# Cosine attention into a leaky-ReLU feed-forward on one core: norms of the second batch moved behind the first batch, two feed-forward groups begun in parts, weights and loads reordered, epsilon added by VectorE

## The chip, the cores and the metric

The kernel runs on one core of a Trainium2 chip. The time is that of one execution on the device, in microseconds (us). The core has five engines with queues of their own: TensorE (PE in the profile), VectorE (DVE), ScalarE (ACT), GpSimd (POOL) and SyncE (SP). Each works through its queue in order; between engines they wait on semaphores.

## The reference

Eight batches of attention with 12 heads, 448 tokens and head dimension 64, with normalised queries and keys, and behind it a feed-forward layer on the 3584 resulting tokens:

```python
q_n = q / (norm(q, axis=-1) + 1e-06)
k_n = k / (norm(k, axis=-1) + 1e-06)
scores = q_n @ k_n.T / tau                     # tau = 0.1
attn = softmax(scores, axis=-1)                # denominator + 1e-09
x = (attn @ v).transpose(0, 2, 1, 3).reshape(8 * 448, 768)
h = x @ w_in                                   # 768 x 2048
out = maximum(0.01 * h, h) @ w_out             # 2048 x 768, float32
```

## The kernel before

**Units of work.** A *slot* is a pair of heads of one batch: six slots to a batch, slots 0 to 11 for the first two batches in one layout ("old"), and from slot 12 (`OLD`) on another layout, in which slots carry queries and keys of two pairs by turns. Two slots of an old batch make one *group* j of four heads, three groups to a batch.

**A slot's path.** `load_qk(s)` issues its DMAs on the SP queue into one of four buffers (`ldp`, `bufs=4`), so slot s+4 can only be loaded once slot s is normalised. `squares(s)` (GpSimd, L208, L201) squares the float32 data; `sums(s)` (VectorE, L222, L216) adds over the head dimension into `ss`; `roots(s)` (ScalarE, L229 to L231) takes the root as Ln and Exp with scale 0.5 and then adds epsilon by an Identity activation; `normalise(s)` (VectorE, L239 and L245 or L255) takes the reciprocal and multiplies into the bf16 tile `qn`; `transposes(s)` turns it (L269 on TensorE and the copy L310 on VectorE for old slots, L291 on VectorE and six stores on SP, L300, for new ones) into `qkT`. `hold(x)` is a GpSimd copy of one column that waits for the norm (L580), so that what follows it on GpSimd does not start earlier.

**Attention.** `scores(s, kis)` multiplies key tiles against all queries (L331) into two PSUM banks, and ScalarE takes the exponential with scale 1/tau (L340); tile 3 of a pair of slots holds the last 64 keys of both. `totals(j)` multiplies the exponentials with ones (L351) and takes Ln and Exp with scale -1 on ScalarE (L362, L363); `products(j, e)` multiplies with the values (L351); `scale(j, e)` (VectorE, L382) writes their product into block 2j+e of six of `xT`. New slots use `quad_tiles` (L402, L408), `group_products` (L427) and `group_scale` (L452).

**Feed-forward.** Chunk c of tokens is 384 columns for an even c and 512 for an odd one. `first(c, m)` multiplies six blocks of `w_in` with `xT` (L474) and puts the leaky ReLU (ScalarE, L480) into `hT`; 16 groups m per chunk. `second(c, ts, half)` multiplies 16 blocks of `hT` with one half of `w_out` (L502), copies the result (VectorE, L513) and stores it. Weights and values come by GpSimd's DMA queue (`load_w_in`, `load_w_out`, `load_v`, `load_v_rem`, `load_vq`).

**Order.** It is written out by hand; the program keeps it engine by engine. `fill(n)` issues n matmuls whose results are not used. The first batch is the loop `for s in range(NPAIR)` (six steps): each step issues the scores of slot s, normalises and transposes slot s+1, loads slot s+5, squares slot s+3, and sums and takes the root for slot s+2; in odd steps the remaining value product and the scaling of an earlier group stand between, in even steps that group's totals and first value product stand behind the transposes. Then `attend(j)` does the last group, and a hand-written prelude (L674 to L712) prepares slots 7 to 10 of the second batch between 13 of the 16 first groups of chunk 0 (`feed_groups`). The table `opened` (L718) orders the rest of the second batch and the rest of chunk 0: its row i names tiles of scores and the slot that is prepared ahead. From L764 on, visits of three tiles each are filled with feed-forward work by cost.

PSUM has eight banks; `banks` deals the oldest, in the first batch score tiles from banks 0 to 3 and everything else from 4 to 7 (`deals["apart"]`).

Of the kernel before, what the change touches and what calls it, by code (L numbers as in the profile page):

```python
# [8 lines left out]
F32 = mybir.dt.float32  # L9
# [7 lines left out]
def kernel(  # L17
# [146 lines left out]
    def load_v_rem(b, heads=range(4)):  # L164
        if b >= B:
            return
        r = v[b, :, MAIN:S].rearrange("(j g) p d -> g p j d", g=4)
        for g in heads:
            lo = 64 * (g // 2)
            gp.dma_start(out=vrb[b % 2][lo : lo + 64, :, g], in_=r[g])  # L170
# [55 lines left out]
    def roots(s):  # L226
        if s >= NSLOT:
            return
        nc.scalar.activation(ss[s], ss[s], func=AF.Ln, bias=tiny)  # L229
        nc.scalar.activation(ss[s], ss[s], func=AF.Exp, scale=0.5)  # L230
        nc.scalar.activation(ss[s], ss[s], func=AF.Identity, bias=eps)  # L231

    qn = {}

    def normalise(s):
        if s >= NSLOT:
            return
        r = smp.tile([128, 14], F32, name="r")
        nc.vector.reciprocal(r, ss[s])  # L239
        if s >= OLD:  # L240


            qn[s] = qnp.tile([128, 7, D, 2], BF16, name="qn")
            t, n = ("(m e)", "(e m)")[s % 2], 2
            nc.vector.tensor_tensor(  # L245
                qn[s].rearrange("p m d e -> p m e d"),
                raw[s].rearrange(f"p ({t[1:-1]} d) -> p m e d", e=n, d=D),
                r.rearrange(f"p {t} -> p m e", e=n).unsqueeze(3).to_broadcast([128, 7, 2, D]),
                op=ALU.mult,
            )  # L250
            return
        qn[s] = qnp.tile([128, 7, 2, D], BF16, name="qn")
        for x, lo, hi, r0 in ((raw[s][0], 0, 4, 0), (raw[s][1], 4, 7, 8)):
            nt = hi - lo
            nc.vector.tensor_tensor(  # L255
                qn[s][:, lo:hi],
                x.rearrange("p h t d -> p t h d"),
                r[:, r0 : r0 + 2 * nt].rearrange("p (h t) -> p t h", h=2)
                .unsqueeze(3).to_broadcast([128, nt, 2, D]),
                op=ALU.mult,  # L260
            )
# [203 lines left out]
    def chunk_cols(c):  # L465
        return (0, MAIN) if c % 2 == 0 else (MAIN, 512)

    def first(c, m):
        c0, n = chunk_cols(c)
        if m == 0:  # L470
            hT[c] = htp.tile([128, MT, 512], BF16, name="hT")
        pm = banks(1)
        for kt in range(KT):
            nc.tensor.matmul(  # L474
                out=pm[:, :n],
                lhsT=w_in_sb[:, kt, m * 128 : (m + 1) * 128],
                rhs=xT[c // 2][:, kt, c0 : c0 + n],
                start=(kt == 0), stop=(kt == KT - 1),
            )
        nc.scalar.activation(out=hT[c][:, m, :n], in_=pm[:, :n], func=AF.Prelu, alpha=0.01)  # L480

    osb = {}
# [65 lines left out]
    load_qk(3)  # L548
    tiny = cpool.tile([128, 1], F32, name="tiny")
    nc.vector.memset(tiny, 1e-18)  # L550
    eps = cpool.tile([128, 1], F32, name="eps")
    nc.vector.memset(eps, 1e-6)
    warm = pep.tile([128, 2 * S], BF16, name="pe")[:, 0:512]
    nc.vector.memset(warm, 1.0)  # L554
    ones = cpool.tile([128, 32], BF16, name="ones")
# [22 lines left out]
    def hold(x):  # L578
        seen = smp.tile([128, 1], F32, name="seen")
        gp.tensor_copy(out=seen, in_=x)  # L580
# [34 lines left out]
    for s in range(NPAIR):  # L615
        j = s // 2 - 1 if s >= 2 else None
        even = s % 2 == 0
        n = s + 2 if s and s + 2 <= NPAIR + 1 else None
        if s == 1:
            roots(2)  # L620
        scores(s, (0,))
        if j is not None and not even:
            products(j, 1)
        scores(s, (1,))
        fill(2)
        if n and n <= NPAIR:
            sums(n, (0,))
        normalise(s + 1)
        load_qk(s + 5)
        if j is not None and not even:  # L630
            scale(j, 0)
        hold(qn[s + 1][:, 6, 0, 0:1])
        squares(s + 3)
        if s == 0:
            sums(2)
            load_v_rem(0, range(2, 4))
        if not even:
            load_v(s // 2 + 1)
        if s != 1 and s < 5:
            load_w_in(max(s - 1, 0))  # L640
        if s == 5:
            load_v_rem(1)
        if n:
            sums(n, (1,) if n <= NPAIR else (0, 1))
        scores(s, (2,))
        if not even or s == 0:
            fill(2)
        if not even:
            scores(s, (3,))
        transposes(s + 1)  # L650
        if not even or s == 0:
            fill(2)
        if n:
            roots(n)
        if j is not None and not even:
            scale(j, 1)
        if j is not None and even:
            totals(j)
            products(j, 0)

    def attend(j):
        totals(j)
# [7 lines left out]
    deals["apart"] = False  # L670
    deals["width"] = 64
    s, j = NPAIR, NQ - 1
    attend(j)
    scores(s, (0, 1))  # L674
    feed_groups(0, 1)
    normalise(s + 1)
    load_qk(s + 5)
    load_w_out(0)
    hold(qn[s + 1][:, 6, 0, 0:1])
    squares(s + 3)  # L680
    sums(s + 2)
    feed_groups(0, 3)
    transposes(s + 1)
    roots(s + 2)
    feed_groups(0, 2)
    scores(s, (2,))
    scores(s + 1, (0,))
    normalise(s + 2)
    load_qk(s + 6)
    hold(qn[s + 2][:, 6, 0, 0:1])  # L690
    squares(s + 4)
    load_v(s // 2 + 1)
    load_w_out(1)
    sums(s + 3)
    roots(s + 3)
    feed_groups(0, 2)
    scores(s + 1, (1, 2))
    normalise(s + 3)
    load_qk(s + 7)
    feed_groups(0, 1)  # L700
    transposes(s + 2)
    sums(s + 4)
    feed_groups(0, 2)
    roots(s + 4)
    scores(s + 1, (3,))
    normalise(s + 4)
    load_qk(s + 8)
    hold(qn[s + 4][:, 6, 0, 0:1])
    squares(s + 5)
    feed_groups(0, 1)  # L710
    transposes(s + 3)
    feed_groups(0, 1)  # L712

# [13 lines left out]
    for i, (at, tiles, ahead) in enumerate(opened):  # L729
        share = (sum(g[0] for g in queue[:-1]) + sum(costs[i:])) / (len(opened) - i) - costs[i]  # L730
        if at is not None:
            attend(b * NQ + at)
            if at == 0:
                load_v(b * NQ + 2)
            else:
                load_vq(0)
        key_tiles([(b * NPAIR + p, ki) for p, ki in tiles])
        done = 0
        s = b * NPAIR + ahead if ahead else NSLOT
        sums(s)  # L740
        roots(s)
        if i < 2:
            if i == 1:
                cost, fn = queue.pop(0)
                fn()
                done += cost
            transposes(NPAIR + 4 + i)
        if s < NSLOT:
            normalise(s)
            if s >= OLD:  # L750
                transposes(s)
            load_qk(s + 4)
            hold(qn[s][:, 6, 0, 0:1])
            squares(s + 1)
        while len(queue) > 1 and (i == len(opened) - 1 or done + queue[0][0] / 2 <= share):
            cost, fn = queue.pop(0)
            fn()
            done += cost
    sums(OLD + 3)
    squares(OLD + 4)  # L760
    roots(OLD + 3)
# [136 lines left out]
```

## Time and profile before

| what | us |
|---|---|
| median of 3 runs (lowest, highest) | 424.99 (424.94, 425.61) |
| the profiled execution | 425.26 |
| its span, first to last instruction | 423.5 |
| TensorE busy | 413.2 |
| ScalarE, VectorE, GpSimd busy | 267.8, 212.0, 114.7 |
| mean granted TensorE clock | 1.000 |

The page gives busy times over the whole span. The 40 digits of its second part are tenths of busy time in slices of 10.6 us each. A timeline lists the instructions of one engine in order of time: start, duration, line, operation, tiles and shapes, number of instructions merged, and in brackets the idle time of the engine before them with what ended it. A line number is that of the kernel that is shown. The landing time of a DMA is counted from its issue.

### The profile page before, as it was taken

What the parts mean: (1) busy time and instruction counts of PE and PEld (TensorE: products, weight loads), DVE (VectorE), ACT (ScalarE), POOL (GpSimd) and SP (SyncE); (2) the same over time, 40 slices, a digit from 0 to 9 for tenths busy, and PEclk for the clock granted to TensorE, in tenths of its full rate; (3) what the DMA queues carried; (4) which work ended last, traced back from release to release, by engine and by line L of the source; (5) the groups of instructions that cost most, each with busy time, mean ns of one, the idle gap of its engine ahead of it and who ended that gap; (6) DMA issues with size and microseconds to landing.
All of it is one profiled execution on the core that took longest, in us unless ns stands there. A gap on an engine that the chain in (4) does not pass through costs nothing.

```text
span 423.5 us, 11361 instructions
## 1 busy us (share of the span) xinstructions
PE 413.2 (98%) x4797; PEld 213.3 (50%) x4797; DVE 212.0 (50%) x335; ACT 267.8 (63%) x478; POOL 114.7 (27%) x150
## 2 busy tenths in 40 slices
PE   8889999999999999999999999999999999999996
PEld 3334555444455555554445555554445555654463
DVE  5877657774667645765564963465411312120021
ACT  3998885688858687758865777657774454104300
POOL 3867533533234132413231432123010000000000
PEclk9999999999999999999999999999999999999999
DMA  6999999765376953574365583543441200010021
GB/s 150 197 233 221 232 233 207 192 198 137 65 184 158 226 134 74 151 187 134 77 159 166 110 237 71 116 125 121 84 88 39 77 37 3 37 76 0 2 74 74
DMA packets 41906, 53.82 MB, mean 127 GB/s; under 512 B 12544, under 2 KB 32256, under 8 KB 41856
## 3 DMA queue, kind: packets, MB, share of 16 engines
q1 hardware_dynamic: 25536, 40.85, 34.0%
q0 software_dynamic: 15488, 11.80, 19.3%
q8 instruction: 37, 0.61, 0.6%
q10 hardware_dynamic: 832, 0.46, 0.4%
q14 instruction: 13, 0.11, 0.1%
HBM read 45.61 MB, written 11.01 MB: 134 GB/s over the span
## 4 chain that ended last, share of the span: by engine, by line
PE 84%; DVE 6%; ACT 4%; DMA 2%; issue 1%; POOL 1%; SPq 0%; POOLq 0%; DVEq 0%
PE ps L474 34%; PE ps L502 31%; PE ps L427 8%; PE ps L402 6%; DMA qk_h<-in_q_dram 2%; PE ps L571 2%; DVE qn L245 1%; ACT pe L340 1%; PE ps L351 1%; DVE ss L216 1%; DVE qn L255 1%; PE ps L331 1%; POOL sq L201 1%; ACT pe L408 1%; PE ps L269 1%
## 5 line engine op out<-in xcount | busy, mean ns | idle before, releaser
L502 PE MATMUL ps<-w_out_sb,hT 128*128 128x384 bf16 x896 | 151.4, 326 | 0.3 <-DVE xT L382 0.2
L474 PE MATMUL ps<-xT,w_in_sb 128*128 128x384 bf16 (+1 forms) x768 | 151.1, 353 | 0.0
L408 ACT ACTIVATE pe<-ps 128x896 bf16<-128x896 f32 x126 | 109.0, 916 | 42.4 <-PE ps L402 40.7
L502 PEld LDWEIGHTS <-hT 128*128 128x128 bf16 x896 | 85.4, 98 | 65.0 <-issue 10.2
L474 PEld LDWEIGHTS <-w_in_sb 128*128 128x128 bf16 x768 | 73.1, 98 | 73.6 <-issue 8.5
L480 ACT ACTIVATE hT<-ps 128x384 bf16<-128x384 f32 (+1 forms) x128 | 67.6, 547 | 59.3 <-PE ps L474 58.9
L513 DVE COPY osb<-ps 128x384 f32<-128x384 f32 (+1 forms) x56 | 30.8, 550 | 107.6 <-PE ps L502 101.9
L201 POOL TENSOR_TENSOR sq<-qk_h 128x896 f32<-128x896 f32 x36 | 60.4, 1678 | 1.6 <-DMA qk_h<-in_k_dram 1.6
L580 POOL CAST seen<-qn 128x1 f32<-128x1 bf16 x47 | 8.6, 183 | 181.3 <-DVE qn L245 168.1
L245 DVE TENSOR_TENSOR qn<-qk_h,r 128x896 bf16<-128x896 f32 x36 | 42.7, 1185 | 1.2
L239 DVE RECIPROCAL r<-ss 128x14 f32<-128x14 f32 x48 | 11.4, 237 | 59.6 <-ACT ss L231 59.6
L402 PE MATMUL ps<-qkT 64*32 64x448 bf16 x1008 | 38.9, 353 | 0.9 <-DVE xT L452 0.4
L340 ACT ACTIVATE pe<-ps 128x896 bf16<-128x896 f32 x42 | 35.8, 916 | 5.0 <-PE ps L331 3.6
L216 DVE TENSOR_REDUCE ss<-sq 128x14 f32<-128x896 f32 x36 | 37.5, 1041 | 2.6 <-POOL sq L201 2.6
L291 DVE STREAM_TRANSPOSE tt<-qn 128x448 f32<-128x448 f32 x36 | 29.6, 824 | 1.2
L452 DVE TENSOR_TENSOR xT<-ps,rb 128x448 bf16<-128x448 f32 x32 | 18.3, 613 | 21.5 <-PE ps L427 21.4
L427 PE MATMUL ps<-pe,vq 64*32 64x448 bf16 x1008 | 27.3, 349 | 0.0
L402 PEld LDWEIGHTS <-qkT 64*32 64x32 bf16 x1008 | 14.1, 91 | 21.9 <-issue 17.1
L208 POOL TENSOR_TENSOR sq<-qk_h 128x384 f32<-128x384 f32 (+1 forms) x21 | 19.5, 945 | 11.6 <-DMA qk_h<-in_k_dram 11.4
L229 ACT ACTIVATE ss<-ss,tiny 128x14 f32<-128x14 f32 x48 | 14.6, 305 | 11.6 <-DVE ss L216 9.2
L427 PEld LDWEIGHTS <-vq 64*32 64x32 bf16 x1008 | 14.7, 92 | 7.8 <-issue 0.3
L571 PE MATMUL ps<-pe 128*128 128x512 bf16 x53 | 17.0, 446 | 1.5 <-DVE pe L554 1.5
(52 smaller groups left out, 218.7 us busy)
## 6 DMA issues: line engine op xcount, KB each, us to landing
qk_h<-in_q_dram SPq DMA_DIRECT2D x36, 224.0 KB, 4.2
qk_h<-in_k_dram SPq DMA_DIRECT2D x36, 224.0 KB, 4.0
out_dram<-osb SPq DMA_DIRECT2D x20, 384.0 KB, 2.5
qkT<-tt SPq DMA_DIRECT2D x72, 56.0 KB, 2.2
qkT<-tt SPq DMA_DIRECT2D x36, 112.0 KB, 2.4
vq<-in_v_dram POOLq DMA_DIRECT2D x16, 224.0 KB, 4.9
w_in_sb<-in_moe_w_in_dram POOLq DMA_DIRECT2D x4, 768.0 KB, 9.9
w_out_sb<-in_moe_w_out_dram POOLq DMA_DIRECT2D x2, 1536.0 KB, 23.4
```

The source lines that it names most:

```text
L201: gp.tensor_tensor(sq, raw[s], raw[s], op=ALU.mult)
L216: nc.vector.tensor_reduce(ss[s], sqs[s].rearrange("p (t d) -> p t d", d=D), axis=AX.X, op=ALU.add)
L245: nc.vector.tensor_tensor(qn[s].rearrange("p m d e -> p m e d"), raw[s].rearrange(f"p ({t[1:-1]} d) -> p m e d", e=n, d=D), r.rearrange(f" ...
L291: nc.vector.transpose(out=to.rearrange(("p g (c m) -> p m g c", "p g (m c) -> p m g c")[which], m=7), in_=qn[s].bitcast(F32).rearrange("p ...
L340: nc.scalar.activation(out=dst, in_=sc[:, :, :S], func=AF.Exp, scale=inv_tau)
L402: nc.tensor.matmul(out=sc[32 * strip : 32 * strip + 32, a, :S], lhsT=x[rows, c0 : c0 + 32], rhs=x[rows, 0:S], start=True, stop=True,)
L408: nc.scalar.activation(out=pq[u, i], in_=sc[:, :, :S], func=AF.Exp, scale=inv_tau)
L427: nc.tensor.matmul(out=po[32 * strip : 32 * strip + 32, w, :S], lhsT=weights, rhs=pq[us[x if two else 0], i][rows, a, :], start=(i == 0), ...
L474: nc.tensor.matmul(out=pm[:, :n], lhsT=w_in_sb[:, kt, m * 128 : (m + 1) * 128], rhs=xT[c // 2][:, kt, c0 : c0 + n], start=(kt == 0), stop= ...
L480: nc.scalar.activation(out=hT[c][:, m, :n], in_=pm[:, :n], func=AF.Prelu, alpha=0.01)
L502: nc.tensor.matmul(out=po2[:, :HALF], lhsT=hT[c][:, m, ts * 128 : (ts + 1) * 128], rhs=w_out_sb[:, m, half * HALF : (half + 1) * HALF], st ...
L513: nc.vector.tensor_copy(out=o[:, half * HALF : half * HALF + cut], in_=po2[:, :cut])
```

## The change

- `roots` loses the Identity activation; `normalise` begins with `tensor_scalar_add` on VectorE, in place on `ss`. The tile `eps` and its memset go.
- `first` can do part of its six blocks: with `hi` below six the PSUM bank is kept in `begun`, and a later call goes on in it.
- In the first batch's loop the sums, roots, norm and transposes of slots 6 and 7 are no longer issued. In odd steps the root stands ahead of the fourth score tile; in even steps totals and the first value product stand ahead of the transposes. In the last step the value loads and the first half of `w_out` stand ahead of slot 8's squares on GpSimd, with no hold there.
- Behind the loop, the last group's totals and products are followed by blocks 0 to 3 of the first two feed-forward groups, then its scaling and the root of slot 6, then blocks 4 and 5. Slots 6 to 10 are prepared between the other groups, each with its sums ahead of the transposes of the slot before. 13 groups are done by the end of this part, as before.
- Loads: slot 10 is issued behind slot 6's norm, slot 11 behind slot 7's, slot 12 behind slot 9's and slot 13 behind slot 10's. In `opened` a row loads slot s+3 in place of s+4, and slot 18 is loaded at its end.

```diff
-        nc.scalar.activation(ss[s], ss[s], func=AF.Identity, bias=eps)
...
         r = smp.tile([128, 14], F32, name="r")
+        nc.vector.tensor_scalar_add(ss[s], ss[s], 1e-6)
         nc.vector.reciprocal(r, ss[s])
...
-    def first(c, m):
+    begun = {}
+
+    def first(c, m, lo=0, hi=KT):
         c0, n = chunk_cols(c)
-        if m == 0:
+        if c not in hT:
             hT[c] = htp.tile([128, MT, 512], BF16, name="hT")
-        pm = banks(1)
-        for kt in range(KT):
+        pm = begun.pop((c, m)) if lo else banks(1)
+        for kt in range(lo, hi):
...
+        if hi < KT:
+            begun[c, m] = pm
+            return
...
-        n = s + 2 if s and s + 2 <= NPAIR + 1 else None
+        n = s + 2 if 0 < s < NPAIR - 2 else None
+        last = s == NPAIR - 1
...
-        normalise(s + 1)
-        load_qk(s + 5)
+        if not last:
+            normalise(s + 1)
+            load_qk(s + 5)
         if j is not None and not even:
             scale(j, 0)
-        hold(qn[s + 1][:, 6, 0, 0:1])
+        if last:
+            load_v(s // 2 + 1)
+            load_v_rem(1)
+            load_w_out(0)
+        else:
+            hold(qn[s + 1][:, 6, 0, 0:1])
         squares(s + 3)
...
+        if n and not even:
+            roots(n)
         if not even:
             scores(s, (3,))
-        transposes(s + 1)
+        if j is not None and even:
+            totals(j)
+            products(j, 0)
+        if not last:
+            transposes(s + 1)
         if not even or s == 0:
             fill(2)
-        if n:
+        if n and even:
             roots(n)
         if j is not None and not even:
             scale(j, 1)
-        if j is not None and even:
-            totals(j)
-            products(j, 0)
...
-    attend(j)
-    scores(s, (0, 1))
+    totals(j)
+    sums(s)
+    po = banks(2)
+    for e in range(2):
+        products(j, e, po[:, e])
+    for m in range(2):
+        first(0, m, 0, KT - 2)
+    for e in range(2):
+        scale(j, e)
+    roots(s)
+    for m in range(2):
+        first(0, m, KT - 2)
+    work[0] = work[0][2:]
+    normalise(s)
+    load_qk(s + 4)
+    hold(qn[s][:, 6, 0, 0:1])
+    squares(s + 3)
+    sums(s + 1)
+    feed_groups(0, 1)
+    transposes(s)
+    roots(s + 1)
     feed_groups(0, 1)
     normalise(s + 1)
     load_qk(s + 5)
-    load_w_out(0)
-    hold(qn[s + 1][:, 6, 0, 0:1])
-    squares(s + 3)
     sums(s + 2)
-    feed_groups(0, 3)
+    scores(s, (0, 1))
+    feed_groups(0, 1)
     transposes(s + 1)
     roots(s + 2)
-    feed_groups(0, 2)
+    feed_groups(0, 1)
...
-            load_qk(s + 4)
+            load_qk(s + 3)
             hold(qn[s][:, 6, 0, 0:1])
             squares(s + 1)
...
+    load_qk(OLD + 6)
     sums(OLD + 3)
```

## The prediction

> **What bounds the kernel now.** I read the page first, then the table of windows, then the timelines of TensorE, VectorE and GpSimd one after the other, and last the landing times of single transfers.
>
> ```profile
> PE 413.2 (98%) x4797; PEld 213.3 (50%) x4797; DVE 212.0 (50%) x335; ACT 267.8 (63%) x478; POOL 114.7 (27%) x150
> ...
> DMA  6999999765376953574365583543441200010021
> ```
> ```profile
> 10.00:20.00 10.00, 8.04 (x56) 2.85 (x53) 8.20 (x18) 9.52 (x19) 9.29 (x13) 1.00 1.01 197
> 20.00:30.00 10.00, 8.32 (x92) 3.27 (x90) 7.55 (x15) 9.61 (x17) 5.94 (x9) 1.00 1.16 224
> 30.00:40.00 10.00, 9.93 (x139) 4.35 (x138) 7.33 (x15) 8.20 (x16) 9.43 (x14) 1.00 1.17 230
> ```
>
> The table has start and end, length, then the busy time of TensorE, its weight loads, VectorE, ScalarE and GpSimd, the clock, the DMA share and GB/s. TensorE is the bound: 413.2 of 423.5 us, at granted clock 1.00 throughout. The built program has exactly the same TensorE work after the change, in another order up to the first batch's end plus some 18 us and in the same order behind it. So only its idle time can be won. That is 1.61 us before 10 us, 1.96 and 1.68 us in the next two windows, then almost none, and 3 us at the end. In 10 to 30 us ScalarE is busy 9.5 of 10, and DMA is full until about 65 us. The timelines name the waits:
>
> ```profile
> 18.25 0.55 PE L331 MATMUL ps<-qkT 64*128 64x448 bf16 x4 [0.29 <-DVE qkT L310]
> ...
> 19.82 0.36 PE L331 MATMUL ps<-qkT 64*128 64x448 bf16 x2 [0.48 <-ACT pe L340]
> ...
> 29.67 0.81 PE L269 MATMUL ps<-id,qn 128*128 128x128 bf16 x7 [1.10 <-DVE qn L255]
> ```
> ```profile
> 26.99 1.82 POOL L208 TENSOR_TENSOR sq<-qk_h 128x512 f32<-128x512 f32 x2 [2.80 <-DMA qk_h<-in_k_dram]
> ```
> ```profile
> 28.06 0.69 DVE L222 TENSOR_REDUCE ss<-sq 128x8 f32<-128x512 f32 x1 [0.76 <-POOL sq L208]
> 28.66 0.23 DVE L239 RECIPROCAL r<-ss 128x14 f32<-128x14 f32 x1
> 28.92 1.16 DVE L255 TENSOR_TENSOR qn<-qk_h,r 128x512 bf16<-128x512 f32 x2
> ```
>
> The longest gap, 1.10 us, is a queue order: the sums of slot 6, which belongs to the second batch, stand on VectorE ahead of slot 5's norm, and they wait for squares that waited for a late load. Behind 30 us the gaps are short:
>
> ```profile
> 74.36 0.38 PE L331 MATMUL ps<-qkT 64*64 64x448 bf16 x3 [0.17 <-DVE osb L513]
> 74.89 2.76 PE L502 MATMUL ps<-w_out_sb,hT 128*128 128x384 bf16 x16 [0.15 <-DVE xT L382]
> 84.23 0.38 PE L402 MATMUL ps<-qkT 64*32 64x448 bf16 x8 [0.36 <-ACT pe L408]
> 136.34 0.38 PE L402 MATMUL ps<-qkT 64*32 64x448 bf16 x7 [0.18 <-DVE xT L452]
> 238.42 0.38 PE L402 MATMUL ps<-qkT 64*32 64x448 bf16 x7 [0.19 <-DVE xT L452]
> ```
>
> With 0.11 us at 61.96 (the first output-weight matmul, whose weights landed at 61.9) this is 1.16 us. All idle behind 10 us, 4.9 us, is the most that there is to win.
>
> **Part 1: epsilon on VectorE.** 48 Identity activations go (0.31 us each, 0.21 to 0.25 to the next start), and 48 additions on 128x14 come. No such operation is in the trace. Memset 128x1 takes 0.06, reciprocal 128x14 takes 0.24; these are the ends. Reduces of 128, 384 and 512 elements take 0.28, 0.55 and 0.68 us, a line that gives 0.16 us at 14 elements, and I take that. For slot 1 the Exp ends at 10.92 and the reciprocal starts at 11.30; with an addition it starts at 10.92+0.04+0.16+0.03 = 11.15, so 0.15 us sooner (0.07 to 0.25). The dropped epsilon memset lets the one that TensorE waits for start up to 0.13 us sooner; I count 0.1. By the Trainium skill, VectorE: DVE Perf Modes, section The TRN2 errata, an SBUF operation costs 58 cycles plus its elements, an estimate of 0.07 us; the sum would then be about 0.2 us better, and no run here shows it.
>
> **Part 2: the first batch's loop.** Two roots, the sums of slots 6 and 7, their norms and transposes leave it. In even steps totals and products now stand ahead of the transposes, and the copy of the transposed tile is the next step's start. I replay the path with row distances. Slot 1's first scores move 0.15+0.1 sooner, its first softmax exponential from 14.85 to 14.60. ScalarE is then gapless over three of them (2.51), a shorter root (0.54, moved ahead of the fourth) and the fourth (0.84): step 2 starts its exponentials at 18.49, before 18.87. From there to step 3's first scores: 0.95 to the third scores (row 18.87 to 19.82), 0.30, totals 0.77, products 0.86, transposes 0.56, copy 0.61, handovers 0.10, together 4.15: 22.64, which is later than before's 22.39. Step 3 is TensorE's own sequence in both, 4.43 (22.39 to 26.82): 27.07. Step 4: 0.40+4.15: 31.62, before 32.04. Step 5 without its transposes (0.39): 32.04 to 36.12 less 0.39 is 3.69, so the last totals start at 35.30, before 36.12. Of this 0.82 us the moved transposes give back 0.39. **Loop: 0.43 us won** (0.2 to 0.65 with the addition's ends). The 1.10 us gap goes, but each even step now ends with 0.88 us in which TensorE waits for transposes and copy.
>
> **Part 3: behind the first batch.** Slot 6's norm now follows the first batch's last scale. The eight matmuls of two groups on the first four blocks of xT (8 x 0.165 = 1.3 us) hide the logarithm, exponential and scale; the remaining four and the third group (1.65 us) hide the norm (0.19+0.27+1.16): 40.16 against transposes at 40.6. Continuing so: scores of slot 6 have 0.1 us in hand, transposes of slots 7, 8, 9 have 0.1, 0.8, 0.25. If all this cover were gone, each norm would cost up to 1.6 us. Three margins under 0.2 us on rows with scatter: **0.1 us lost** (0 to 1.3, below).
>
> **Part 4: queues and loads.** On GpSimd the first half of w_out is issued at about 36.2 instead of 38.81, ahead of slot 8's squares (4.5 us of issues now precede them, unused until slot 8's sums), and nothing on TensorE waits for those. With its 23.1 us from issue to landing it lands at 59.3, ahead of its use at 61.5; 0.11 us won at 61.96. The second half is now issued behind slot 10's squares, at 50.5 to 51.5 instead of 49.92; its row, 23.6 us, would land it at 74.1 to 75.1, and it is used at 74.3. But that row holds the waiting behind the first half (landed 61.9), which now ends 2.6 us sooner: I count 0, with 0.8 lost as the other end. The loads of slots 10 and 11 move behind their norms: slot 10 from 33.4 to about 40.2. Loads 14 to 18 come one step later; on SP slot 16 now stands behind six stores of transposed tiles (74.0 to 78.5) and lands near 82, while its sums are due at 85.4: hidden, and if not, up to 3 us on VectorE ahead of the chain at 84. Later gaps: at 84.23 ScalarE's shorter root (0.25) leaves 0.11 of 0.36. At 136 and 238 the chain runs through the Identity; 0.15 each. At 74 the norm in front is held by VectorE's own queue and the addition returns what the Identity gave: 0. **Later: 0.11+0.25+0.30 = 0.66 won** (0.9 won to 0.3 lost).
>
> **Sum.** -0.43+0.1-0.66 = -0.99 us on the profiled execution (span 423.5, time 425.26, so 1.76 around it). Its time stands 0.27 above the median 424.99; taken off the median: 424.0.
>
> **Rivals.**
> Late loads (slower, 0.14). The root of slot 10 stands on ScalarE ahead of the last softmax tile that the totals of the batch's second group need at 54.7. Backwards: exponential 0.9, root 0.54, sums 1.07, squares 1.82: slot 10 must have landed by 50.4, 8 to 10 us after its issue at 40.2 to 42.3. Landing times in us are last in these rows (issued about 34 and 42):
>
> ```profile
> qk_h<-in_k_dram SPq DMA_DIRECT2D x1, 192.0 KB, 12.6
> ```
> ```profile
> qk_h<-in_k_dram SPq DMA_DIRECT2D x1, 192.0 KB, 8.0
> ```
>
> With 12.6 it comes at 52.6 to 54.7, TensorE stands 2.2 to 4.3 us: about 427. For it: DMA is full there. Against: that row had a second load in front and w_in in flight, which is gone at 43.7.
>
> Squares beside norms (0.18):
>
> ```profile
> 44.28 2.27 POOL L208 TENSOR_TENSOR sq<-qk_h 128x512 f32<-128x512 f32 x2 [3.18 <-DMA qk_h<-in_k_dram]
> ```
> ```profile
> 44.69 2.27 DVE L255 TENSOR_TENSOR qn<-qk_h,r 128x512 bf16<-128x512 f32 x2
> ```
>
> Side by side a norm takes 1.1 us more than alone. After the change slot 8's squares (37.3 to 39.1) meet slot 6's addition and norm, and slot 10's may meet slot 9's. Less the margins 0.45 and 0.25 that is 0.5 and 0.85 us: 424.5 to 425.4, and up to 425.9 if slot 7 is caught too. The Trainium skill, SBUF — State Buffer, section Who interferes with whom, calls this an exclusive lock for the whole instruction, under which the new addition would be held as well; the two rows agree for the norm.
>
> The idle only moves (0.10): the even steps' late transposes cost all that the loop won, later gains stay at half: 424.6.
>
> More is won (0.08): the even steps' 0.88 us is partly covered and the short gaps close: about 422.9.
>
> **Numbers.** Forecast 0.50, its own range 423.3 to 424.5, with 0.08 of it above 424.14. About 0.2%, 0.85 us, is what a measurement can tell here. Faster: 0.42+0.08 = 0.50. Within: 0.08, squares 0.13, idle moves 0.10 = 0.31. Slower: loads 0.14, squares' end 0.05 = 0.19. The range 423.0 to 425.8 leaves out the late loads and the far end of the larger win.
>
> **What would show it.** Right: the last totals start near 35.3; no wait of the transposes for the norm at step 4, but 0.8 us waits of scores for the copy at steps 3 and 5; additions near 0.16; no TensorE gap over 0.3 us between 36 and 60. Wrong: gaps at the transposes of slots 6 to 9, norm pairs over 1.5 us, ScalarE's root waiting for slot 10's sums near 52, or a loop that ends later than 35.9.

## The result, and the profile after

| what | before | after |
|---|---|---|
| median, us (13 runs each, taken by turns) | 425.57 | 427.57 |
| lowest, highest | 424.76, 427.40 | 426.59, 428.69 |
| the profiled execution, and its span | 425.26, 423.5 | 426.59, 424.8 |

The ratio is 1.0049 (95% interval 1.0034 to 1.0064): 0.5% slower. The forecast was 424.0 us, faster, with a range up to 425.8. In some executions of the kernel before, the mean granted clock is 0.991 to 0.996 and the time about 2 us longer (last section), so beside some medians below stands that of the executions at 0.999 or more ("at full clock"), which for the kernel before is 424.8 to 425.0 in every later set. The changed kernel is 2.6 to 2.7 us above that.

The page of the changed kernel, engines and DMA, against the two lines shown of before:

```profile
PE 411.5 (97%) x4779; PEld 213.6 (50%) x4797; DVE 221.6 (52%) x382; ACT 255.5 (60%) x430; POOL 114.8 (27%) x149
...
DMA  6899999875375963575375583544441100010021
```

VectorE took over what ScalarE gave up (+9.6 us, -12.3 us); DMA is as full up to 65 us as it was. The table of windows, from 10 to 30 us:

```profile
10.00:20.00 10.00, 8.10 (x52) 2.73 (x51) 8.87 (x20) 8.54 (x16) 9.14 (x13) 1.00 0.90 168
20.00:30.00 10.00, 8.57 (x103) 3.62 (x107) 7.83 (x17) 8.83 (x15) 5.82 (x9) 1.00 1.16 229
```

ScalarE is no longer full between 10 and 30 us (8.5 and 8.8 for 9.5 and 9.6). TensorE's timeline, the waits that answer to those shown of before:

```profile
14.78 0.55 PE L331 MATMUL ps<-qkT 64*128 64x448 bf16 x4 [0.81 <-ACT ss L230]
18.58 0.36 PE L331 MATMUL ps<-qkT 64*128 64x448 bf16 x2 [0.29 <-DVE qkT L310]
23.16 0.36 PE L331 MATMUL ps<-qkT 64*128 64x448 bf16 x2 [0.72 <-DVE qkT L310]
32.17 0.36 PE L331 MATMUL ps<-qkT 64*128 64x448 bf16 x2 [0.72 <-DVE qkT L310]
75.26 0.97 PE L507 MATMUL ps<-w_out_sb,hT 128*128 128x384 bf16 x5 [0.15 <-DVE xT L382]
88.60 0.35 PE L402 MATMUL ps<-qkT 64*32 64x448 bf16 x1 [1.26 <-DVE xT L382]
89.13 0.76 PE L402 MATMUL ps<-qkT 64*32 64x448 bf16 x23 [0.18 <-DVE xT L382]
137.73 0.38 PE L402 MATMUL ps<-qkT 64*32 64x448 bf16 x7 [0.18 <-DVE xT L452]
239.73 0.38 PE L402 MATMUL ps<-qkT 64*32 64x448 bf16 x7 [0.18 <-DVE xT L452]
```

The wait of 1.10 us at 29.67 is gone, and the two of 0.72 for the copy of transposed tiles are there. The wait of 0.36 at 84 is gone, and one of 1.26 us at 88.60 has come. Ahead of it lies this on VectorE, GpSimd and SP of the changed kernel:

```profile
83.44 1.46 DVE L238 TENSOR_SCALAR ss<-ss 128x14 f32<-128x14 f32 x1 [0.62 <-ACT ss L230]
84.93 0.24 DVE L239 RECIPROCAL r<-ss 128x14 f32<-128x14 f32 x1
85.21 1.17 DVE L245 TENSOR_TENSOR qn<-qk_h,r 128x896 bf16<-128x896 f32 x1
```
```profile
83.19 1.68 POOL L201 TENSOR_TENSOR sq<-qk_h 128x896 f32<-128x896 f32 x1 [2.14 <-DMA qk_h<-in_q_dram]
```
```profile
74.37 3.79 SPq L300 DMA_DIRECT2D qkT<-tt  x6
...
78.67 0.52 SPq L136 DMA_DIRECT2D qk_h<-in_q_dram  x1
```

and this on SP and GpSimd of the kernel before (the squares of slots 15 and 16 in one run):

```profile
67.72 1.10 SPq L136 DMA_DIRECT2D qk_h<-in_q_dram  x2
```
```profile
79.03 3.31 POOL L201 TENSOR_TENSOR sq<-qk_h 128x896 f32<-128x896 f32 x2
```

Read backwards: slot 16's load is issued at 78.67, behind the six stores (67.72 before). Its squares run from 83.19 to 84.87 (they were over at 82.34 before). Slot 15's addition starts at 83.44 and ends at 84.90, when the squares end: 1.46 us for an instruction that elsewhere takes 0.17. The same shows at the start: slot 1's addition ends with slot 2's squares, 11.66 against 11.63.

```profile
10.81 0.85 DVE L238 TENSOR_SCALAR ss<-ss 128x14 f32<-128x14 f32 x1 [0.35 <-ACT ss L230]
15.23 0.17 DVE L238 TENSOR_SCALAR ss<-ss 128x14 f32<-128x14 f32 x1
```
```profile
9.81 1.82 POOL L208 TENSOR_TENSOR sq<-qk_h 128x512 f32<-128x512 f32 x2
```

The span, cut at marks on TensorE (us; the loop begins here with slot 1's first scores):

| stretch | before | after |
|---|---|---|
| to the first transposes | 9.34 | 9.18 |
| to slot 1's first scores | 5.11 | 5.60 |
| loop, to the first batch's last totals | 21.67 | 21.08 |
| to the second batch's first totals | 18.47 | 19.19 |
| to its last totals | 26.51 | 26.42 |
| to the first group with 512 columns | 7.21 | 8.58 |
| to the end | 335.19 | 334.75 |

Of the fourth row 0.39 us is the transposes that were moved there. The last two waits that the prediction wanted shorter, at 137 and 239, did not change.

### The profile page after: what moved, and what is told of

The parts are those of the page before. It is cut to its first block, busy times and chain, and to the rows that moved or that the text cites. A ratio compares the mean times of both kernels' runs of the same rounds, so it can differ in the third digit from the quotient of the medians.

```text
span 424.8 us, 11331 instructions
## 1 busy us (share of the span) xinstructions
PE 411.5 (97%) x4779; PEld 213.6 (50%) x4797; DVE 221.6 (52%) x382; ACT 255.5 (60%) x430; POOL 114.8 (27%) x149
## 4 chain that ended last, share of the span: by engine, by line
PE 82%; DVE 8%; ACT 4%; DMA 3%; issue 2%; SPq 0%; POOL 0%; ACTq 0%; POOLq 0%; DVEq 0%
PE ps L476 32%; PE ps L507 31%; PE ps L427 8%; PE ps L402 6%; DMA qk_h<-in_k_dram 2%; PE ps L351 2%; PE ps L331 2%; DVE ss L216 1%; DVE qn L245 1%; DMA qk_h<-in_q_dram 1%; ACT pe L340 1%; ACT pe L408 1%; PE ps L269 1%; DVE ss L238 1%; DVE xT L382 1%
## 5 line engine op out<-in xcount | busy, mean ns | idle before, releaser
L201 POOL TENSOR_TENSOR sq<-qk_h 128x896 f32<-128x896 f32 x36 | 60.5, 1680 | 3.1 <-DMA qk_h<-in_q_dram 2.1
L238 DVE TENSOR_SCALAR ss<-ss 128x14 f32<-128x14 f32 x48 | 11.0, 230 | 49.1 <-ACT ss L230 48.8
L208 POOL TENSOR_TENSOR sq<-qk_h 128x384 f32<-128x384 f32 (+1 forms) x21 | 19.5, 945 | 12.7 <-DMA qk_h<-in_k_dram 12.6
L331 PE MATMUL ps<-qkT 64*64 64x448 bf16 (+1 forms) x132 | 13.4, 361 | 4.1 <-DVE qkT L310 2.0
```

The lines of the kernel that those rows point to most:

```text
L201: gp.tensor_tensor(sq, raw[s], raw[s], op=ALU.mult)
```

## The experiments

**The changed kernel again, and two parts of it undone one at a time.** `e0` is the changed kernel, `e1` gives epsilon back to ScalarE, `e2` issues the loads of slots 12 to 18 as early as before, `e3` keeps epsilon on VectorE as a reduce over pairs.

> The changed kernel once more, unaltered, beside the others, since its profiled execution (426.59 us) was the shortest of its 13 and the median was 427.57. If the traced waits are the whole cause, a second profile shows the same three long additions (0.85 us at slot 1, 0.46 at slot 6, 1.46 at slot 15) and a span of 424.8 to 425.9, and what the longer executions have more must stand as a further wait between 36 and 90 us. If the extra microsecond is not tied to the change, the waits are the same and every stage is a little longer.

Measured: 427.48 (ratio 1.005, 1.003 to 1.007). In this execution slot 1's addition was not held (0.17 us), slot 15's took 1.62 us (TensorE's wait at 88.83: 1.41), and TensorE waited 0.96 us at 62.76 for the output weights. The wait at 88 (1.01 to 1.41 us) is in all five traces that have both the addition and the late load; the others come and go.

```diff
+        nc.scalar.activation(ss[s], ss[s], func=AF.Identity, bias=eps)
...
-        nc.vector.tensor_scalar_add(ss[s], ss[s], 1e-6)
```

> The changed kernel with epsilon added on ScalarE by the Identity activation as before; all else as changed. Theory held additions (an addition on VectorE waits until a running GpSimd instruction ends): the gap of 1.26 us at 88.6 goes, the 0.36 us gap behind the longer root at 84 returns, the loop ends as before at 35.8 (0.68 us of the held addition against 0.25 us per Identity), span about 423.9, 0.9 us below the changed kernel. Rival late load (slot 16's late squares themselves are the stall): the gap at 88 stays over 1 us, span 424.6 or more. Rival order (the new order of the loop and behind it costs the time): about 424.8 in both places.

Measured: profiled 425.64 and span 423.9, but median 427.38 (1.0051, 1.0034 to 1.0069). Without the addition the late squares of slot 16 (82.58 to 84.26) meet slot 15's norm, on VectorE, and TensorE still waits:

```profile
83.46 1.82 DVE L245 TENSOR_TENSOR qn<-qk_h,r 128x896 bf16<-128x896 f32 x1
```
```profile
87.51 0.35 PE L402 MATMUL ps<-qkT 64*32 64x448 bf16 x1 [0.41 <-DVE xT L382]
```

So of the 1.44 us at 88 (1.26 and 0.18) 0.59 comes without the addition too, from a norm of 1.82 in place of 1.17; 0.85 more comes where the addition is what is held. What the Identity costs stands against it: the loop is 21.31 us in place of 21.08, and the wait of 0.36 at 84 is back, so 0.26 is left to be won. The median shows none of it (427.38 for 427.48), and it lies 1.7 us above this trace, the lowest of eleven executions: a cause stays open that this trace does not have.

```diff
+    load_qk(s + 6)
...
-            load_qk(s + 3)
+            load_qk(s + 4)
...
-    load_qk(OLD + 6)
```

> The changed kernel with the loads of slots 12 to 18 at their former places (slot s+4 behind slot s's norm); the additions stay on VectorE. Held additions: slot 16's squares follow slot 15's at about 81 and are over by 82.7, slot 15's addition at 83.4 takes 0.17 us instead of 1.46, the gap at 88.6 goes (-1.4 us), the 0.85 us addition of slot 1 stays and the last totals start at 35.9 as before; span about 423.4. Late load: the same at 88. Order: no more than 0.3 us better.

Measured: 426.65 (1.0026, 1.0008 to 1.0044). The wait at 88 is gone (0.18 left), 0.83 us of the median won. Additions are still held at other places, up to 0.85 us, and slot 7's norm takes 1.46 us at 43.70 with a wait of 0.33 at the transposes behind it.

In `e3` each element of `pairs` holds a root and, beside it, epsilon; the lines that make these tiles are left out here:

```diff
...
-        nc.vector.tensor_scalar_add(ss[s], ss[s], 1e-6)
-        nc.vector.reciprocal(r, ss[s])
+        nc.vector.tensor_reduce(r, pairs[s % 4], axis=AX.X, op=ALU.add)
+        nc.vector.reciprocal(r, r)
```

> The changed kernel with its late loads, but epsilon is added by a VectorE reduce over pairs (sum, epsilon) instead of a tensor_scalar. Held additions, if it is the form of the instruction that is held: the reduces take about 0.17 us each beside running squares too, slot 1's scores start at 14.1 instead of 14.78, the last totals at 35.2, the gap at 88.6 goes although slot 16's squares still run at 83.2 to 84.9; span about 422.7, below before's 423.5. Late load: the gap at 88.6 stays over 1 us, span 424.1 or more. Order: 424.8.

Measured: 426.68 (1.0025, 1.0008 to 1.0042), 0.80 us less than `e0`. The 48 reduces take 178 ns in the mean. At slot 15, VectorE and then GpSimd:

```profile
83.77 0.18 DVE L244 TENSOR_REDUCE r<-pair 128x14 f32<-128x28 f32 x1 [0.62 <-ACT pair L236]
83.99 0.24 DVE L245 RECIPROCAL r<-r 128x14 f32<-128x14 f32 x1
84.27 1.83 DVE L251 TENSOR_TENSOR qn<-qk_h,r 128x896 bf16<-128x896 f32 x1
```
```profile
83.39 1.68 POOL L207 TENSOR_TENSOR sq<-qk_h 128x896 f32<-128x896 f32 x1 [2.03 <-DMA qk_h<-in_q_dram]
```

The reduce and the reciprocal pass beside the squares; now the norm behind them is held, 1.83 for 1.17 us, as in `e1`. TensorE waits 0.64 instead of 1.26. The reduce reads twice what the addition reads and is not held: it is the kind of instruction that decides, not its size.

**The parts alone, and two together.** `e4` is the kernel before with the addition on VectorE, `e7` the kernel before with the later loads; `e5` and `e6` are `e3` and `e1` with the loads as before, so `e6` is the reordering alone.

> The kernel before with the epsilon moved to VectorE and nothing else. Held additions: at slot 1 the addition comes at 10.8 while slot 2's squares run (9.96 to 11.78) and takes 0.7 to 1.0 us instead of 0.17, the first scores of slot 1 start at 14.7 to 14.9 instead of 14.45, one or two more are held between 39 and 55 us; 0.2 to 0.8 us slower than before. Were an addition only its 0.17 us, the kernel would be 0.2 to 0.5 us faster, through the gaps at 84, 136 and 238.

Measured: 425.93 (1.0017, 0.9993 to 1.004), 424.92 at full clock, as the kernel before. On balance the addition alone costs nothing: where it is held most (0.89 us at 44.10) TensorE does not wait behind it, and at slot 1, where a hold was expected, it took 0.23 in this execution.

> The changed kernel with both repairs: epsilon by the reduce, and the loads of slots 12 to 18 at their former places. If held additions and the late slot-16 load are the two causes and add up (0.85 us each by the medians), 425.8 us median, no gap at 88, within 0.2% of before. If they are one cause seen twice (either repair frees the gap at 88), 426.6 as with one alone.

Measured: 425.68 (1.0015, 0.9995 to 1.0035): both cures together win 1.8 us from the changed kernel (427.48). Its trace, of a longer execution (426.54), has a norm of 2.01 us beside squares near 43.6 and a wait of 0.72 us at the transposes behind it.

> The reordering alone: epsilon on ScalarE as before and the loads of slots 12 to 18 at their former places. If late loads make the spread of the version with the Identity (425.6 to 428.6), its runs lie within 1 us of each other and near 425.5; the gap at 87 goes. If the reordering itself costs, the median stays at 427.

Measured: 425.86 (1.0016, 0.9994 to 1.0037), 425.78 at full clock. The reordering alone is no gain, and 0.9 us worse than the kernel before at full clock.

> The kernel before with only the loads of slots 12 to 18 one step later, as in the change. Late load: slot 16's squares run at 82.5 to 84.2 instead of 80.7 to 82.3, its sums stand ahead of the scale that TensorE waits for, a gap of 0.4 to 0.6 us at 87.5, span about 424.0, median 425.6 or more with a wider spread. If the loads are hidden in this order: 425.0 and no gap at 87.

Measured: 426.21 (1.0016, 0.9993 to 1.0039), 425.42 at full clock, 0.5 us worse. Its trace has what was expected at this place: slot 15's norm takes 1.77 us beside the late squares, and TensorE waits 0.36 and 0.18 us at 89. The rest of that trace, of an execution with a lowered clock, is read in the last section.

**The load ahead of the stores.** In `opened` the load was put ahead of the six stores, still one step later than before.

```diff
+            load_qk(s + 3)
             if s >= OLD:
                 transposes(s)
-            load_qk(s + 3)
```

> The changed kernel with one line moved: in the table that orders the rest of the second batch, a row's load stands ahead of the six stores of transposed tiles on SP instead of behind them. All loads stay one step later than in the kernel before. Theory A (slot 16's load stands behind six stores, so its squares end at 84.9 and hold slot 15's addition): load issued near 68, squares end near 83, the addition takes 0.2 us in place of 1.46, TensorE's wait of 1.26 us near 88.6 goes to under 0.4, the stretch from the last old group's totals to the first group of chunk 1 falls from 8.6 to about 7.3 us; median about 426.5, as with all loads put back. Theory B (it is the loads of slots 12 to 15 that cost, by their transfers): the wait near 88 goes, but the median stays above 427.1.

Measured: 426.45 (1.0025, 1.0008 to 1.0042). Slot 16's load is issued at 68.94, its squares are done at 83.3, and the wait at 88 is 0.19. Slot 15's addition:

```profile
84.14 0.17 DVE L238 TENSOR_SCALAR ss<-ss 128x14 f32<-128x14 f32 x1 [0.62 <-ACT ss L230]
```

One line was worth 1.0 to 1.1 us of the median (427.48 in `e0`, 427.57 at first): theory A.

> The same move of one line, and epsilon added by ScalarE's Identity again. With the Identity alone put back the median was 427.38, with the loads put back as well 425.86. Theory A (the six stores ahead of slot 16's load are all of that 1.5 us): about 425.9. Theory B (the other later loads cost): about 427. In both no addition is held on VectorE.

Measured: 426.72 (1.0032, 1.0015 to 1.0049), between the two theories: five executions at 425.4 to 426.1, seven at 426.7 to 428.1. If these are two bunches, and not only a wide scatter, neither theory has them: something happens in some executions and not in others.

**Where the kernel before could win.** In the kernel before, step 4's sums of slot 6 were put behind slot 5's norm:

```diff
-        if n and n <= NPAIR:
+        if n and n <= NPAIR and s != 4:
             sums(n, (0,))
         normalise(s + 1)
+        if s == 4:
+            sums(n, (0,))
```

> The kernel before with one thing moved: in step 4 of the first batch's loop the first half of slot 6's sums stands behind slot 5's norm on VectorE, not ahead of it. Theory (the 1.10 us wait at 29.67 is only this queue order): the norm starts at 27.4 in place of 28.66, TensorE's wait falls from 1.10 to about 0.3, the stretch from slot 1's scores to the last totals from 21.67 to about 20.9, and nothing is given back behind it, since slot 6's root comes no later; about 424.3, ratio 0.998. Rival (the gain is lost again where slot 6's products on TensorE or its root wait): the stretch is shorter, the time unchanged at 425.1.

Measured: 424.66 (0.9985, 0.9972 to 0.9999), lowest 424.08 and highest 424.95; against the kernel before at full clock, 424.84 in this set, that is 0.2 us. The loop went from 21.67 to 20.41 us, and then:

```profile
61.69 1.47 PE L502 MATMUL ps<-w_out_sb,hT 128*128 128x384 bf16 x8 [1.36 <-DMA w_out_sb<-in_moe_w_out_dram]
```

1.26 us won in the loop, 1.25 lost again at the landing of the first output weights (a wait of 1.36 for 0.11).

> The same move, and epsilon added by VectorE in the form of a reduce over pairs whose second element is the constant (the Identity on ScalarE goes). Theory (the reduce isn't held by GpSimd, and ScalarE's root is 0.25 us shorter): the waits at 84, 136 and 238 close by 0.1 to 0.25 us each, about 423.9, ratio 0.997. Rival (the reduce's 0.2 us on VectorE gives back what the Identity gave on ScalarE): as the move alone, 424.3.

Measured: 424.61 (0.9977, 0.9961 to 0.9993), with a wait of 1.24 us for the same weights. It can't be told from `e10`; both are the fastest versions of this case.

> The kernel before with the norm of slot 5 first, as in the run ahead of it, and the values and the first half of the output weights issued ahead of slot 8's squares on GpSimd, so about 4.5 us sooner. There the loop's stretch from slot 1's scores to the last totals was 20.41 in place of 21.67 us, but TensorE then waited 1.36 us for the first output weights at 61.69, and the time was 424.66. Theory (what the loop wins is lost to the landing of the output weights, which bounds this part in every kernel of the case): the wait falls to 0.5 or less, the time to about 423.8. Rival (DMA is full there, so an earlier issue lands no sooner): the wait stays over 1 us, the time at 424.7.

Measured: 424.96 (0.9995, 0.9978 to 1.0012). The weights were issued at 37.64 instead of 39.44 and landed at 62.4 instead of 61.6:

```profile
62.52 0.66 PE L502 MATMUL ps<-w_out_sb,hT 128*128 128x384 bf16 x3 [1.23 <-DMA w_out_sb<-in_moe_w_out_dram]
```

The wait and the time are those of the rival: 1.80 us sooner in issue was not sooner in landing. As a rule that is too strong: over all twenty traces these weights are issued at 35.2 to 40.8 and land at 59.6 to 62.9, and the ten issued before 37 land about a microsecond sooner in the median (60.5) than the six issued after 38.5 (61.7), with a scatter of 3 us among the ten.

**Three more traces.**

> The changed kernel once more, for a second trace, since the two traced executions (426.59 and 426.81) lie below the median of 427.5. Theory W (output weights): the wait ahead of the first second-layer matmul near 62.7, 0 and 0.96 in the two traces, is 1 us or more. Theory S (slot 16): the wait near 88.6 is over 1.5 us. Theory K (the late slots 10 and 11): a wait over 0.3 us at the transposes or totals between 45 and 56. Each says which of the three is longer here than in the first trace, by what the execution is longer.

Measured: 425.93, of one execution. The wait at 87.90 is 1.11 us, none is over 0.3 between 36 and 62.

> The changed kernel a third time, with the same three theories: the wait that grows with the execution's time is near 62.7 (W), near 88.6 (S) or between 45 and 56 (K).

Measured: 427.86, 1.93 us more. Its stretch from the first batch's last totals to the second's first is 20.55 us, against 19.00 in `e13` and 19.19 in the first trace: theory K by place, though not by slots 10 and 11. GpSimd, VectorE and TensorE in this execution:

```profile
43.17 2.27 POOL L208 TENSOR_TENSOR sq<-qk_h 128x512 f32<-128x512 f32 x2 [1.70 <-DMA qk_h<-in_k_dram]
```
```profile
43.38 2.47 DVE L255 TENSOR_TENSOR qn<-qk_h,r 128x512 bf16<-128x512 f32 x2
```
```profile
44.81 0.40 PE L269 MATMUL ps<-id,qn 128*128 128x128 bf16 x4 [0.29 <-DVE qn L255]
45.91 0.34 PE L269 MATMUL ps<-id,qn 128*128 128x128 bf16 x3 [0.70 <-DVE qn L255]
```

and GpSimd and VectorE at the same place in the first trace:

```profile
43.80 2.24 POOL L208 TENSOR_TENSOR sq<-qk_h 128x512 f32<-128x512 f32 x2 [2.51 <-DMA qk_h<-in_k_dram]
```
```profile
43.20 1.16 DVE L255 TENSOR_TENSOR qn<-qk_h,r 128x512 bf16<-128x512 f32 x2
```

Slot 9's squares start when slot 9's load lands. Where that is 0.21 us ahead of slot 7's norm, the norm takes 2.47 us and the transposes wait; where it is 0.60 us behind, the norm takes 1.16 and GpSimd pays. The traces of `e2`, `e5` and `e8` have the same meeting (norms of 1.46, 2.01 and 2.26 us; in `e2` the addition is held for 0.60 as well), and the same stretch takes 20.26, 20.69 and 20.35 us there. The kernel before has one too, the norm of 2.27 us that the prediction shows at 44.69, but TensorE does not wait there. What differs is the cover: 0.1 us at slot 7 by the prediction's own count.

> Identity on ScalarE and loads one step later, with the load ahead of the stores, for a second trace: its executions fall into two bunches (425.4 to 426.1 and 426.7 to 428.1) and the traced one, 425.39, was the lowest. Theory W: where it takes over 426.7, TensorE waits a microsecond or more for the output weights near 62. Theory K: it waits between 45 and 56.

Measured: 425.47, again of the lower bunch, with no wait over 0.27 between 36 and 84. It tells nothing of the upper one. Slot 6's norm meets slot 8's squares in it (2.00 us).

**The meeting taken away.** The hold ahead of slot 9's squares waits for slot 7's norm instead of slot 6's, and the squares move with it; nothing else moves.

```diff
-    hold(qn[s][:, 6, 0, 0:1])
-    squares(s + 3)
     sums(s + 1)
...
     load_qk(s + 5)
+    hold(qn[s + 1][:, 6, 0, 0:1])
+    squares(s + 3)
     sums(s + 2)
```

> The changed kernel with one thing moved: GpSimd's hold ahead of slot 9's squares waits for slot 7's norm, not slot 6's, so that these squares can't run beside slot 7's norm. In the four traces of the changed kernel they started at 43.17 to 44.52, when slot 9's load had landed; where they started 0.21 us ahead of slot 7's norm, that norm took 2.47 in place of 1.16 us, TensorE waited at the transposes near 45, and the execution took 427.86; in the others it took 425.93 to 426.81. Theory (this meeting, decided by a landing, is the microsecond that the median has over the lucky traces): slot 7's norm takes 1.16, the stretch from the last totals of the first batch to the first of the second is 19.0 to 19.2, no executions stand near 428, the median is about 426.4. Rival (it isn't this): the median stays at 427.5.

Measured: 426.52 (1.0024, 1.0006 to 1.0042); eleven of twelve executions at 426.36 to 427.08. GpSimd and VectorE:

```profile
44.60 1.82 POOL L208 TENSOR_TENSOR sq<-qk_h 128x512 f32<-128x512 f32 x2
```
```profile
43.19 1.16 DVE L255 TENSOR_TENSOR qn<-qk_h,r 128x512 bf16<-128x512 f32 x2
```

One microsecond of the median is gone, and most of the scatter with it (425.69 to 429.06 in `e0`). This meeting was the open cause.

> The same move, with epsilon added by ScalarE's Identity again and a row's load ahead of its six stores. Without the move the executions fell into two bunches, 425.4 to 426.1 and 426.7 to 428.1, median 426.72. Theory: only the lower bunch is left, median about 425.6, within 0.2% of the kernel before; the loop's 0.2 us that are left after the moved transposes don't show. Rival: both bunches stay, median 426.7.

Measured: 425.82 (1.0001, 0.9985 to 1.0017), eleven of twelve executions at 425.13 to 426.39; of the upper bunch one at its edge, 426.71, is left. Beside the kernel before at full clock, 424.96 in this set, it is still 0.9 us longer. In its trace slot 6's norm meets slot 8's squares (2.00 us for 1.16 at 39.49), and the stretch behind the first batch is 19.66, as in `e15`; in `e1` and `e9`, where that norm takes 1.16, it is 18.97.

## Why the prediction was wrong

Three steps of it failed: the cost of the addition, the load of slot 16 that was called hidden, and a margin of 0.1 us at slot 7. The replay of the loop was right.

**The loop: right.** From slot 1's first scores to the last totals the replay gave 21.10 (14.20 to 35.30); measured were 21.08, 21.09, 21.08 and 21.09 in the first trace, `e0`, `e13` and `e14`. The two waits of scores for the copy were given as 0.8 and are 0.72. That 0.39 us goes back with the moved transposes was right too. The start was not: slot 1's scores came at 14.43 to 14.91 in these four. Part of that is scatter (13.92 to 14.51 in the four traces with before's start), part the first step below.

**Part 1, the addition: the first step that failed.** Its own price was right, 0.17 for 0.16 us; the 0.07 that stood beside it was too low. The ends of its cost, 0.06 and 0.24, were those of instructions that run alone. In the profiled execution it also took 0.85, 0.46, 0.72 and 1.46, each time until a GpSimd instruction ended. So the failed step is the cost: a hold that the sum put at nothing. The prediction had the rule beside it and left it to a rival: the Trainium skill, SBUF — State Buffer, section Who interferes with whom, calls the shared port pair of VectorE and GpSimd an exclusive lock that the second one waits for, names tensor_scalar among the operations that can take it, and says that tensor_reduce never contends. The runs agree: 1.46 for the addition beside squares, 0.178 in the mean for the reduce. Norms are held in the runs too (1.83 in `e3`). `e4` shows that the hold costs nothing by itself; it needs a place without cover. Slot 1's and slot 15's are such places: from the first transposes to slot 1's scores it is 5.59 or 5.60 us in the four traces in which that addition takes 0.85, and 5.17 to 5.29 in three of the same loop in which it takes 0.17 to 0.25.

**Part 4, slot 16's load: the second, called hidden.** The stores were at 74.4 to 78.2 (74.0 to 78.5 given), the landing at about 82.1 to 83.2 (82 given), and the squares ended at 84.87, ahead of the sums at 86.98. So the sums of slot 16 were not late, as said. What was not asked is what the squares would meet on their way: slot 15's addition and norm, behind which stand the scalings that TensorE needs at 88. There 1.44 us were lost (1.26 and 0.18) where nothing had been counted. `e8` shows it by one line: 1.0 to 1.1 us of the median. The 0.11 us to be won by the output weights depends on their landing: at 60.9 in the profiled execution, with no wait, and at 62.7 in `e0`, with 0.96.

**Part 3, the margins: the third.** It counted norms at 1.16 us, gave slot 7's transposes 0.1 us in hand, and put the squares beside norms into a rival for slots 8 and 10. The squares that decided were slot 9's, since their start is not set by a queue but by a landing, in `e14` 11.1 us after the issue. So the failed step is that 0.1 us in hand, a margin smaller than what a meeting costs. 0.1 us lost was counted; it is 0.1 in `e13`, 0.3 in the first trace and 1.7 in `e14` (20.55 less 18.47 and 0.39), where 1.6 had been named for a norm without cover. The rival had the right mechanism; its 424.5 to 425.9 were too low because they kept the gains of the other steps and held no addition at slot 15.

**The later waits: one right, two wrong.** At 84 the wait of 0.36 is in every trace with the Identity and in none with the addition or the reduce; 0.25 of it had been counted as won. At 136 and 238, 0.15 each was to be won because the chain ran through the Identity. It doesn't: the waits are 0.18 and 0.18 or 0.19 with it (before, `e1`, `e6`) and without (after, `e3`, `e4`). And every trace without the Identity has a wait of 0.17 or 0.18 at 172 to 176 that none has with it. So, net, 0.2 us was won by the shorter root at the later waits (0.36 less 0.17), for the 0.55 given.

**Late slots 10 and 11: the rival was right in part.** Slot 10's squares waited 3.67 us for the load (up to 8.9 us from issue to landing, inside the 8.0 to 12.6 taken), slot 10's sums were late, and ScalarE waited 2.13 us for them ahead of its root at 54.04. TensorE did not wait there, so the late loads cost nothing in this trace. The output weights' second half was issued at 54.18, 3 us later than given, and landed at 73.0 all the same.

**The sum.** -0.99 was predicted and +1.3 came in the span of the profiled execution: start +0.33, loop -0.59, behind the first batch +0.72, from there to the first group with 512 columns +1.28, the rest -0.44 (a stretch of 334.7 to 335.2 us in all twenty traces, so scatter at least in part). The median adds to it what that execution did not have, the meeting at slot 7. Of the 0.9 us of `e17`, slot 6's norm is 0.7 in its trace (19.66 less 18.97); what is left stays open.

## What to carry to other kernels

A step that is moved to a place where it is not late by its own use can still be late by what it meets: list for its new time which instructions of VectorE and GpSimd lie beside it, and price each with up to the whole of the other's duration. Where an instruction's start is set by a landing and not by a queue, its neighbours change between executions, so one profiled execution gives one of several cases; hold it behind the work that it must not meet, as one line did here for a microsecond. Before winning time on TensorE, look up the next landing that it runs towards: here 1.26 us won in the loop stopped at output weights that landed at 59.6 to 62.9 us, whether they were issued at 35.2 or at 40.8.

## What the runs showed of the hardware

**The clock after a wait.** In the trace of `e7`, whose loop is that of the kernel before, the wait for slot 5's norm (the one of 1.10 us at 29.67 before) was 1.86 us. TensorE's timeline, and the table of windows with the clock third from the end of each line:

```profile
29.91 0.97 PE L269 MATMUL ps<-id,qn 128*128 128x128 bf16 x7 [1.86 <-DVE qn L255]
30.81 1.31 PE L351 MATMUL ps<-pe,ones 128*32 128x448 bf16 x12
```
```profile
26.00:28.00 2.00, 1.42 (x9) 0.41 (x8) 0.78 (x2) 1.94 (x6) 0.78 (x1) 1.00 1.15 223
28.00:30.00 2.00, 0.14 (x4) 0.10 (x3) 1.68 (x4) 1.25 (x2) 2.00 (x4) 0.92 1.11 228
30.00:32.00 2.00, 2.00 (x23) 1.03 (x27) 1.65 (x4) 0.83 (x3) 0.74 (x2) 0.50 1.21 233
32.00:34.00 2.00, 2.00 (x30) 0.73 (x26) 1.43 (x3) 1.18 (x3) 1.30 (x1) 0.73 1.25 200
```

Twelve totals take 1.31 us instead of 0.75 at a clock of 0.50. Behind 1.10 us in the trace of before and 1.49 in that of `e4` the clock stayed at 1.00, so the wait alone does not decide it. Of 144 executions of the kernel before in the later sets, 41 had a mean clock of 0.991 to 0.996; their median is 426.89, that of the 95 at full clock 424.85. Of the two other kernels with the loop as before (`e4`, `e7`) it was 11 of 24. With the norm first (`e10`, `e11`, `e12`) it was 1 of 36, with the new loop (the changed kernel and its nine variants that were timed) 1 of 132. Together, 52 of 168 executions with that wait and 2 of 168 without it. So taking that wait away also takes away the lowered clock, in the executions that had it: an effect that the prediction did not price, and that a median shows only in part (424.90 to 425.57 in the six sets, for 424.85). The Trainium skill, TensorE: Matmul & The Clock Gate, part 1 on the clock gate, says that the clock halves after an idle window of about 3.4 us, and that the windows run freely. The half clock, and that only some executions have it, agree with the runs; it lasts about 3.4 us here (worked out from 0.92, 0.50 and 0.73 in the three windows from 28 to 34). A whole idle window of that length does not: the wait is 1.86 us, and TensorE is busy for 1.56 of the 4 us from 26 to 30.

**A DMA issue can hold VectorE as well.** Slot 10's addition took 0.72 us at 54.63 and ended at 55.35, 0.01 us after GpSimd's issue of the output weights (54.18, 1.16 us). In `e0`, `e2`, `e8`, `e13`, `e14` and `e16` it took 0.72 as well; the reduce of `e3` at this place took 0.18. Not every issue does it: beside the issues of the values' remainders (`load_v_rem`) the additions at 7.95 and 15.23 took 0.17. What tells the two apart is not shown.
